# The first loads of a fused attention and gated-MLP kernel, moved from two issuing engines to one

## The chip, the cores and the metric

The kernel runs on one core of a Trainium2 chip. The metric is the device time of one execution in microseconds (us), the median over several executions. Beside it stands one execution recorded by the hardware profiler; all times inside the kernel come from that record and are counted from the start of its span.

The engines are named as in the profile: PE is TensorE (matmuls), PEld its weight loads, DVE is VectorE, ACT is ScalarE, POOL is GpSimd and SP is SyncE, which computes nothing here and issues DMAs. An entry such as SPq or ACTq is the issue of a DMA by that engine; L540 is line 540 of the kernel.

## What is computed

One sequence x of 2048 rows and 512 columns (bfloat16) is normalised row by row. A local attention (32 heads of 16 columns, 8 positions back at a stride of 2) and a gated MLP with spatial mixing both work on the normalised rows, and x is added to their sum. Cut to what matters here:

```
xn = layernorm(x)
q, k, v = xn @ wqkv                     # 512 x 1536; v is the last third
o = softmax(q . k over 8 dilated positions) applied to v
A = o @ wo
z = gelu(xn @ w_in)                     # 512 x 1792
g = w_sp @ layernorm(z[:, 896:]) + b_sp # mixing over the 2048 rows
B = (z[:, :896] * g) @ w_out
result = x + A + B
```

## The kernel before

The rows are cut into 16 blocks of 128 (block b is rows 128b to 128b + 127). The work goes in stages that overlap: the head, in which the blocks are loaded, normalised and transposed and the first products V and z2 are made; Q, K, the attention's logits and its softmax; z1; the mixing matrix (L982, the longest part); the output product (L1038 and L1047).

Each piece of work is a task with its engine, what it reads and writes, an estimated duration and a priority. A planner (`Plan.schedule`, L123) plays the tasks through and so fixes each engine's order; `Plan.emit` (L270) then writes the instructions with the semaphore waits that the reads and writes ask for. A DMA task has the engine that issues it as its engine. For some DMAs the planner doesn't work out when they land but is told it by a table of due times in nanoseconds, `land`, at L1094. The lists at L1078 to L1088 force an order by hand on top of that: the whole order of TensorE's tasks in the head, from the warm-up matmuls to the first chunk of Q and K, is one such list, and so is VectorE's.

What the head does, in order:

- TensorE runs warm-up matmuls on a constant (L582, `warm0` to `warm6`, six with 512 columns and then one with 128), which need no load.
- Block 0 of x (L563), block 1 and the next ones (`ld_x`, L536), and the weights of V in two halves (`ld_wv`, L540, 256 of the 512 input rows each) are loaded. Behind them come the two halves of the z2 part of w_in (L546 and L552, called w_in2 here), then block 4.
- For blocks 0 to 2, TensorE transposes the raw block with matmuls against an identity (`pe_tr`, L601, tasks `xTx0a` to `xTx2`); ScalarE copies the result from PSUM to SBUF (L628 for the first two quarters of block 0, L632 for the rest); TensorE multiplies it with V's weights (L704, tasks `V0_0`, `V0_0b` and so on: the first two with the first half of the weights, `V0_1` with the second). The eighth warm-up matmul, `warm7`, stands between block 0's transposes and `V0_0`. ScalarE scales V by the row's reciprocal deviation (L712); what the mean adds is corrected later.
- Meanwhile VectorE makes the statistics of each block (L621, L623, L636), GpSimd the reciprocal deviation (L638), and VectorE the normalised block (L650). Block 0's is transposed by TensorE (`xTr0`, also L601), that of every other block by a DMA transpose that SyncE issues (L644, `xTd1` on).
- TensorE then multiplies the normalised blocks with the second half of w_in (L836, `z2_0_0` on): the first half of block 0's columns needs the first half of w_in2, the second half of the columns the second, and block 1's needs `xTd1`.

Before the change, ScalarE issues block 0 and then block 1, and its next task is a four-element activation (L586), ahead of which it loads its function table. SyncE issues V's weights (both halves), blocks 2 and 3, w_in2's two halves, block 4, and later the DMA transposes. Each of the two engines issues its DMAs one after the other on a queue of its own (q10 for ScalarE, q1 for SyncE in the profile).

Of the kernel before, what the change touches and what calls it, by code (L numbers as in the profile page):

```python
# [346 lines left out]
def build_kernel(nc, A_x, A_wqkv, A_wo, B_x, B_w_in, B_w_sp, B_b_sp, B_w_out, out, report=False, emit=True):  # L347
# [14 lines left out]
    x2 = A_x[0]  # L362
# [48 lines left out]
    with ExitStack() as es:  # L411
# [5 lines left out]
        def A(name, n, o2_=0):  # L417
            return ar[:, off[name] + o2_: off[name] + o2_ + n]

        def AC(o_, dims):  # L420
            return bass.AP(tensor=ar, offset=o_, ap=[[AR, 128]] + [list(d) for d in dims])
# [91 lines left out]
        def dma(eng, fn, nbytes, chan, reads=(), writes=(), name="", xbar=False, prio=0.0, after=()):  # L513
            return T(eng, fn, reads=reads, writes=writes, name=name, prio=prio, after=after,
                     dma=dict(chan=chan, nbytes=nbytes, xbar=xbar, iss=(1270.0 if nbytes < 400000 else 2200.0) if xbar else None))
# [18 lines left out]
        def ld_x(b, eng="sp"):  # L534
            sl = b
            return dma(eng, lambda e: e.dma_start(A("xin", 512, 512 * sl), x2[128 * b:128 * b + 128, :]), 128 * 512 * 2,  # L536
                ("xin", sl), writes=[("xin", sl)], name="ldx%d" % b)

        def ld_wv(hf):
            dma("sp", lambda e: e.dma_start(AC(off["wv"] + 1024 * hf, [[512, 2], [1, 512]]),  # L540
                                            A_wqkv[256 * hf:256 * hf + 256, 1024:1536].rearrange("(c p) n -> p c n",
                                                                                               p=128)),
                256 * 512 * 2, ("wv", hf), writes=[("wv", hf)], name="ldwv%d" % hf)
# [13 lines left out]
        def ld_wqk(which, eng):  # L557
# [2 lines left out]
                A_wqkv[:, 512 * which: 512 * which + 512].rearrange("(c p) n -> p c n", p=128)),  # L560
                512 * 512 * 2, ("wqk", which), writes=[("wqk", which)], name="ld%s" % ("qk"[which]))

        dma("act", lambda e: e.dma_start(A("xin", 512), x2[0:128, :]), 128 * 512 * 2, ("xin", 0),  # L563
            writes=[("xin0", 0), ("xin0", 1)], name="ldx0")
        ld_x(1, "act")
        ld_wv(0)
        ld_wv(1)
        ld_x(2, "sp")
        ld_x(3, "sp")
# [508 lines left out]
        for names in (["warm%d" % wi for wi in range(NWARM)] +  # L1078
# [10 lines left out]
            for n0, n1 in zip(names, names[1:]):  # L1089
                if byname[n0] not in byname[n1].deps:  # L1090
                    byname[n1].odeps.add(byname[n0])

        plan.schedule(tol=4.0, dma_bw=285.0, dma_lat=1600.0, overlap=60.0,
                      land=dict(ldx0=3600.0, ldwv0=4120.0, ldx1=4550.0, ldwv1=5230.0, ldx2=5600.0, ldwin2a=7650.0, ldx3=6050.0,  # L1094
                                ldwin2b=8950.0, csa=75800.0, csb=78400.0, csc=83400.0, csr=86500.0, ldx4=9100.0, ldx5=18150.0, ldq=16300.0, xTd3=12130.0, ldk=17800.0, ldx6=18500.0, ldx7=18900.0, xTd4=13900.0, xTd1=9600.0, xTd2=10850.0, ldwin1=21500.0))
        if report:
            print("arena", AR, "fp", FR)
# [17 lines left out]
def bass_parallel_sum__sliding_local_dilated__mixer_gmlp__prompt_kernel(  # L1115
    nc, A_x, A_wqkv, A_wo, B_x, B_w_in, B_w_sp, B_b_sp, B_w_out, out
):
    build_kernel(nc, A_x, A_wqkv, A_wo, B_x, B_w_in, B_w_sp, B_b_sp, B_w_out, out)
# [28 lines left out]
```

## Time and profile before

| | |
|---|---|
| median of 3 runs | 236.16 us (235.97 to 236.21) |
| the profiled execution's own time | 236.12 us |
| its span | 234.9 us |
| TensorE busy | 98% of the span |
| VectorE busy | 88% |
| ScalarE busy | 41% |
| moved by SyncE's queue (q1) | 41.94 MB |
| moved by ScalarE's queue (q10) | 0.30 MB |

The profiled execution's time is longer than the span by what lies before the first and behind the last instruction that the span holds. Busy time counts an instruction from its start to its end, and since matmuls are pipelined, a busy TensorE can still run below its best rate. The chain of waits follows the last instruction back to whatever released it, step by step. Of a DMA the profile shows the instruction that issues it, on the issuing engine, and the time from there until it has landed.

### The profile page before, as it was taken

To read this page: it belongs to the slowest core of one execution; us is meant where nothing else is said; L and a number is where in the kernel's file an instruction comes from. 1 tells how busy PE (TensorE), PEld (TensorE's weight loads), DVE (VectorE), ACT (ScalarE), POOL (GpSimd) and SP (SyncE) were. 2 spreads that over 40 slices of the span, in tenths; PEclk is the share of its full clock that TensorE was granted. 3 is DMA by queue.
4 is the path that set the end of the run, shared out by engine and by line. 5 is a ranking of instruction groups with operands and counts; after the bars stand their busy time and mean duration, and the time that the engine had idled before them with its cause. 6 is when DMAs were issued, how large, how long until landed. Compare 5 with 4: busy or idle time off the path is not lost.

```text
span 234.9 us, 2982 instructions
## 1 busy us (share of the span) xinstructions
PE 230.9 (98%) x1107; PEld 109.0 (46%) x1127; DVE 207.2 (88%) x271; ACT 96.0 (41%) x144; POOL 29.3 (12%) x58
## 2 busy tenths in 40 slices
PE   8999999999999999999999999999999999999996
PEld 3545455544444444444444444444444444444443
DVE  4706899999999999999999999998899998999723
ACT  3798878888986589510020532011111111000000
POOL 2305640404261202000000000000000000000000
DMA  6769934999811275345299999999969959945442
GB/s 205 219 197 372 175 68 99 217 190 226 230 47 47 67 238 170 63 123 147 74 358 219 282 208 260 190 230 274 300 187 273 305 138 307 290 116 156 112 137 68
DMA packets 83991, 44.55 MB, mean 190 GB/s; under 512 B 56180, under 2 KB 83204, under 8 KB 83976
## 3 DMA queue, kind: packets, MB, share of 16 engines
q1 hardware_dynamic: 82744, 41.94, 70.6%
q0 software_dynamic: 800, 2.11, 2.9%
q10 hardware_dynamic: 432, 0.30, 0.4%
q8 instruction: 9, 0.15, 0.3%
q14 instruction: 6, 0.05, 0.1%
HBM read 26.62 MB, written 4.22 MB: 131 GB/s over the span
## 4 chain that ended last, share of the span: by engine, by line
PE 98%; issue 1%; DVE 0%; DVEq 0%
PE ps L982 41%; PE ps L728 12%; PE ps L836 10%; PE ps L882 10%; PE ps L1047 10%; PE ps L704 6%; PE ps L1038 6%; PE ps L582 1%; PE ps L772 1%; PE ps L601 1%; DVE arena L1053 0%; PE ps L783 0%; DVEq L325 0%
## 5 line engine op out<-in xcount | busy, mean ns | idle before, releaser
L982 PE MATMUL ps<-arena 128*128 128x512 bf16 x439 | 96.6, 379 | 0.5
L982 PEld LDWEIGHTS ps<-arena 128*128 128x128 bf16 x448 | 43.7, 98 | 53.1 <-issue 0.4
L990 ACT ACTIVATE arena<-ps 128x1024 bf16<-128x1024 f32 (+1 forms) x16 | 14.7, 917 | 76.9 <-PE ps L982 70.5
L749 DVE TENSOR_TENSOR arena<-arena 128x4096 bf16<-128x4096 bf16 x16 | 36.5, 2285 | 0.0
L1010 DVE TENSOR_TENSOR arena<-arena 128x4096 bf16<-128x4096 bf16 x16 | 36.5, 2286 | 0.0
L1013 DVE TENSOR_TENSOR arena<-arena 128x2048 bf16<-128x2048 bf16 (+1 forms) x32 | 30.1, 953 | 0.2
L728 PE MATMUL ps<-arena 128*128 128x512 bf16 x124 | 28.2, 379 | 0.3 <-issue 0.2
L754 DVE TENSOR_TENSOR arena<-arena 128x4096 bf16<-128x4096 bf16 x12 | 27.5, 2290 | 0.1
L1047 PE MATMUL ps<-arena 128*128 128x512 bf16 (+2 forms) x116 | 26.5, 366 | 0.1
L836 PE MATMUL ps<-arena 128*128 128x448 bf16 x128 | 25.5, 352 | 0.0
L882 PE MATMUL ps<-arena 128*128 128x512 bf16 x110 | 24.4, 379 | 0.1
L728 PEld LDWEIGHTS ps<-arena 128*128 128x128 bf16 x128 | 14.4, 113 | 13.3 <-ACT arena L718 0.4
L737 ACT ACTIVATE arena<-ps 128x1024 bf16<-128x1024 f32 x16 | 16.2, 1021 | 6.9 <-PE ps L728 6.8
L1053 DVE TENSOR_TENSOR arena<-ps,arena 128x512 bf16<-128x512 f32 (+2 forms) x17 | 11.2, 659 | 8.6 <-PE ps L1047 8.5
L836 PEld LDWEIGHTS ps<-arena 128*128 128x128 bf16 x128 | 12.5, 98 | 12.1
L1047 PEld LDWEIGHTS ps<-arena 128*128 128x128 bf16 x119 | 11.4, 98 | 12.8
L882 PEld LDWEIGHTS ps<-arena 128*128 128x128 bf16 x112 | 11.0, 98 | 13.2
L1038 PE MATMUL ps<-arena 128*128 128x512 bf16 (+2 forms) x68 | 16.6, 366 | 0.1
L704 PE MATMUL ps<-arena 128*128 128x512 bf16 x62 | 16.2, 391 | 0.1
L844 ACT ACTIVATE arena<-ps 128x896 bf16<-128x896 f32 x16 | 14.6, 913 | 3.4 <-PE ps L836 3.3
L621 DVE BATCH_NORM_STATS2 fpool<-arena 128x6 f32<-128x512 bf16 x16 | 10.7, 685 | 5.8 <-DMA arena<-in_A_x_dram 5.8
L888 ACT ACTIVATE arena<-ps 128x1024 bf16<-128x1024 f32 (+1 forms) x16 | 14.0, 919 | 4.4 <-PE ps L882 4.3
(65 smaller groups left out, 168.5 us busy)
## 6 DMA issues: line engine op xcount, KB each, us to landing
arena<-vscr SPq DMA_DIRECT2D x16, 1024.0 KB, 6.2
arena<-in_A_x_dram SPq DMA_DIRECT2D x30, 128.0 KB, 3.9
vscr<-arena POOLq DMA_DIRECT2D x16, 128.0 KB, 4.0
out_dram<-arena SPq DMA_DIRECT2D x15, 128.0 KB, 2.0
arena<-in_A_wqkv_dram SPq DMA_DIRECT2D x2, 512.0 KB, 4.5
arena<-in_B_w_in_dram SPq DMA_DIRECT2D x2, 448.0 KB, 5.1
arena<-in_B_w_in_dram SPq DMA_DIRECT2D x1, 896.0 KB, 8.3
arena<-in_B_w_out_dram SPq DMA_DIRECT2D x1, 896.0 KB, 5.6
```

Of the source, the lines that this page charges most:

```text
L704: last = t.matmul(P(bk, 512), A("xcT", 128, 512 * b + 128 * dc) if b < NRAW else xTv(b, dc), A("wv", 512, 512 * dc), start=(dc == 0), stop ...
L728: last = t.matmul(P(bk, 512, 512 * which), AC(off["wqk"] + 2048 * which + 512 * dc + c, [[4, 128]]), AC(off["xnT"] + dc * S + 512 * j, [[1 ...
L737: T("act", lambda a: a.activation(AC(qo, [[ko - qo, 2], [1, 512]]), P(bk, 1024).rearrange("p (t n) -> p t n", t=2), ACTF.Copy, scale=0.5), ...
L749: T("dve", (lambda pbv, qb, kb: lambda v: v.tensor_tensor(pbv, qb, kb, ALU.mult))(pbv, qb, kb), reads=rd, writes=[("pb", s_)], est=c_tt(40 ...
L754: T("dve", (lambda av, bv: lambda v: v.tensor_tensor(av, av, bv, ALU.add))(av, bv), reads=[("pb", 1)], writes=[("pb", acc)], est=c_tt(4096 ...
L836: last = t.matmul(P(bk, 448, 512 * hf), xTv(b, dc), AC(off["w_in2"] + 896 * dc + 448 * hf, [[1, 448]]), start=(dc == 0), stop=(dc == 3))
L882: last = t.matmul(P(bk, 512, 512 * i), AC(off["w_in1"] + 896 * dc + 128 * fc, [[1, 128]]), AC(off["xnT"] + dc * S + 512 * j, [[1, 512]]), ...
L982: last = t.matmul(P(bk, 512, 512 * i), AC(off["z2"] + FH * sh + 128 * fc, [[1, 128]]), AC(off["wT%d" % r_] + sh * 512, [[1, 512]]), start= ...
L1010: T("dve", lambda v: v.tensor_tensor(tv, tv, av, ALU.mult), reads=[("attn", b)], writes=[("Vs", sv)], est=c_tt(4096), name="pv%d" % b, pri ...
L1013: T("dve", (lambda n: lambda v: v.tensor_tensor(A("Vs", n, 4096 * sv), A("Vs", n, 4096 * sv), A("Vs", n, 4096 * sv + n), ALU.add))(n), wri ...
L1038: last = t.matmul(P(bk, cn), AC(off["OT"] + 512 * tb + 128 * cc, [[1, 128]]), AC(off["wo"] + 512 * cc + c0, [[1, cn]]), start=(cc == 0), s ...
L1047: last = t.matmul(P(bk, cn), AC(off["z1T"] + fc * S + 128 * tb, [[1, 128]]), AC(off["w_out"] + 512 * fc + c0, [[1, cn]]), start=False, sto ...
```

## The change

Block 0 and block 1 are issued by SyncE instead of ScalarE, and the order on SyncE is now block 0, V's weights first half, block 1, V's weights second half, and behind these, as before, blocks 2 and 3, w_in2's halves and block 4. ScalarE issues no load in the head. In the planner's table the due time of block 0 goes from 3600 to 3400; the others stay.

```diff
-        dma("act", lambda e: e.dma_start(A("xin", 512), x2[0:128, :]), 128 * 512 * 2, ("xin", 0),
+        dma("sp", lambda e: e.dma_start(A("xin", 512), x2[0:128, :]), 128 * 512 * 2, ("xin", 0),
             writes=[("xin0", 0), ("xin0", 1)], name="ldx0")
-        ld_x(1, "act")
         ld_wv(0)
+        ld_x(1, "sp")
         ld_wv(1)
         ld_x(2, "sp")
         ld_x(3, "sp")
...
-                      land=dict(ldx0=3600.0, ldwv0=4120.0, ldx1=4550.0, ldwv1=5230.0, ldx2=5600.0, ...
+                      land=dict(ldx0=3400.0, ldwv0=4120.0, ldx1=4550.0, ldwv1=5230.0, ldx2=5600.0, ...
```

More of the change, by code (lines that the diff above doesn't have):

```diff
@@ L1093, in build_kernel @@
         plan.schedule(tol=4.0, dma_bw=285.0, dma_lat=1600.0, overlap=60.0,
-                      land=dict(ldx0=3600.0, ldwv0=4120.0, ldx1=4550.0, ldwv1=5230.0, ldx2=5600.0, ldwin2a=7650.0, ldx3=6050.0,
+                      land=dict(ldx0=3400.0, ldwv0=4120.0, ldx1=4550.0, ldwv1=5230.0, ldx2=5600.0, ldwin2a=7650.0, ldx3=6050.0,
                                 ldwin2b=8950.0, csa=75800.0, csb=78400.0, csc=83400.0, csr=86500.0, ldx4=9100.0, ldx5=18150.0, ldq=16300.0, xTd3=12130.0, ldk=17800.0, ldx6=18500.0, ldx7=18900.0, xTd4=13900.0, xTd1=9600.0, xTd2=10850.0, ldwin1=21500.0))
```

## The prediction, made before the changed kernel was run

> **What bounds the kernel now.** I read the profile's head and its chain first, then TensorE's own timeline over the first 10 us, then the loads.
>
> ```profile
> span 234.9 us, 2982 instructions
> PE 230.9 (98%) x1107; PEld 109.0 (46%) x1127; DVE 207.2 (88%) x271; ACT 96.0 (41%) x144; POOL 29.3 (12%) x58
> PE 98%; issue 1%; DVE 0%; DVEq 0%
> ```
>
> TensorE is 98% of the chain that ended last. So nearly every wait that matters has to be a hole in TensorE's stream, and a load counts only if TensorE reaches its data before the data is there. The change touches loads that are all landed by 9.1 us, so I look for holes there. The next rows are from the timeline (start, length, instructions):
>
> ```profile
> 0.84 2.82 PE L582 MATMUL ps<-const-bfloat16-1.0 128*128 128x512 bf16 x7 [0.84 <-PEq L1132]
> 2.92 0.74 PE L582 MATMUL ps<-const-bfloat16-1.0 128*128 128x512 bf16 x2
> 3.54 0.69 DVE L621 BATCH_NORM_STATS2 fpool<-arena 128x6 f32<-128x512 bf16 x1 [2.35 <-DMA arena<-in_A_x_dram]
> 3.65 0.26 PE L601 MATMUL ps<-arena 128*128 128x128 bf16 x1
> 3.95 0.28 ACT L628 ACTIVATE arena<-ps 128x128 bf16<-128x128 f32 x1 [0.71 <-PE ps L601]
> 4.03 0.31 PE L582 MATMUL ps<-const-bfloat16-1.0 128*128 128x128 bf16 x1
> 4.34 0.21 PEld L704 LDWEIGHTS ps<-arena 128*128 128x128 bf16 x2 [0.27 <-issue]
> 4.37 0.58 PE L704 MATMUL ps<-arena 128*128 128x512 bf16 x1
> 5.18 0.63 PE L601 MATMUL ps<-arena 128*128 128x128 bf16 x4
> 5.61 0.85 PE L704 MATMUL ps<-arena 128*128 128x512 bf16 x2
> 6.03 0.42 PE L704 MATMUL ps<-arena 128*128 128x512 bf16 x1
> 6.29 0.39 PE L601 MATMUL ps<-arena 128*128 128x128 bf16 x4
> 6.51 1.03 PE L704 MATMUL ps<-arena 128*128 128x512 bf16 x4
> 8.46 4.70 PE L836 MATMUL ps<-arena 128*128 128x448 bf16 x24
> ```
>
> Matmul lengths overlap (they hold a pipeline tail), so I go by starts. Four things are seen. First, early 512-column matmuls are 0.43 us apart (5.61 to 6.03) and 128-column ones 0.11 (4 in 5.18 to 5.61); the matmul that starts at 6.03 is followed after 0.26 us, and the group from 8.46 needs 4.70/24 = 0.20 for 448 columns. So the rate doubles inside the matmul from 6.03: with 0.43 us for a slow and 0.22 for a fast one, 0.08 us of its 0.26 were slow, which puts the **rate step** at about 6.11. Second, the last warm-up matmul (128 columns, it starts at 2.92 + 0.43 = 3.35) gives the array free at 3.46; the first transpose of x block 0 starts at 3.65. These 0.19 us are a wait for block 0, which VectorE's statistics show as well (released by the DMA at 3.54). Third, a second hole lies between the last warm-up (4.03 + 0.11 = 4.14) and V's first matmul at 4.37: that one is the transpose's copy by ScalarE (3.95 to 4.23). Fourth, from 4.37 on TensorE runs through.
>
> Now the loads, first their issues (timeline), then issue to landing (DMA view, in windows holding one or two issues):
>
> ```profile
> 0.80 0.43 ACTq L563 DMA_DIRECT2D arena<-in_A_x_dram  x1
> 0.80 0.97 SPq L540 DMA_DIRECT2D arena<-in_A_wqkv_dram  x2
> 1.25 0.46 ACTq L536 DMA_DIRECT2D arena<-in_A_x_dram  x1
> 1.82 0.93 SPq L536 DMA_DIRECT2D arena<-in_A_x_dram  x2
> 2.79 0.43 SPq L546 DMA_DIRECT2D arena<-in_B_w_in_dram  x1
> 3.27 0.51 SPq L552 DMA_DIRECT2D arena<-in_B_w_in_dram  x1
> 3.82 0.51 SPq L536 DMA_DIRECT2D arena<-in_A_x_dram  x1
> ```
>
> ```profile
> arena<-in_A_wqkv_dram SPq DMA_DIRECT2D x1, 256.0 KB, 3.2
> arena<-in_A_x_dram ACTq DMA_DIRECT2D x1, 128.0 KB, 2.7
> arena<-in_A_wqkv_dram SPq DMA_DIRECT2D x1, 256.0 KB, 4.0
> arena<-in_A_x_dram ACTq DMA_DIRECT2D x1, 128.0 KB, 3.1
> arena<-in_B_w_in_dram SPq DMA_DIRECT2D x1, 448.0 KB, 5.5
> arena<-in_A_x_dram SPq DMA_DIRECT2D x1, 128.0 KB, 5.3
> arena<-arena SPq DMA_TRANSPOSE x1, 2.7
> ```
>
> Adding issue and landing time: block 0 lands at 3.5, V's first half at 4.0, block 1 at 1.25 + 3.1 = 4.35, the second half at 1.3 + 4.0 = 5.3, the second half of w_in2 at 3.27 + 5.5 = 8.8, block 4 at 3.82 + 5.3 = 9.1. They already land in the order of the change, though issued by two engines.
>
> **The change part by part.** (a) ScalarE loses two issues (0.43 and 0.46 us). Behind them stands only its table load and a four-element activation; its first copy waits for TensorE until 3.95. Worth nothing.
>
> (b) SyncE gains two issues. Its seven issues are (3.82 - 0.80)/6 = 0.50 apart, so block 0 goes at 0.80, V's first half at 1.30 (0.50 later than now), block 1 at 1.81 (0.56 later), the second half at 2.31, and all behind it about 1.0 later, up to block 4 at 4.82. Whether a later issue is a later landing depends on whether the DMA engines are the limit. The windows view (length, busy times, clock, DMA share, GB/s):
>
> ```profile
> 1.80:2.50 0.70, 0.70 (x4) 0.15 (x1) 0.00 (x0) 0.70 (x1) 0.00 (x0) 1.00 0.72 221
> 2.50:3.50 1.00, 1.00 (x4) 0.29 (x2) 0.00 (x0) 0.73 (x2) 0.00 (x0) 1.00 0.91 304
> 3.50:4.50 1.00, 0.97 (x8) 0.61 (x7) 0.89 (x3) 0.55 (x3) 0.00 (x0) 1.00 0.99 342
> 4.50:5.60 1.10, 1.10 (x6) 0.62 (x6) 1.03 (x5) 0.17 (x1) 0.57 (x1) 1.00 0.91 286
> 5.60:9.70 4.10, 4.10 (x27) 2.21 (x26) 3.30 (x12) 3.15 (x8) 1.76 (x3) 1.00 0.88 282
> ```
>
> From 2.5 on they are 88 to 99% busy: the bytes set the landings, not the issues. I assume the same stream of bytes in the new order. Running sums are 155 kB by 2.5, 459 by 3.5, 801 by 4.5, 1116 by 5.6. Block 0 (131 kB) has passed at 1.80 + 131/221 = 2.39, V's first half (393) at 3.28, block 1 (524) at 3.69, the second half (786) at 4.46. Today the second half lands 5.3 - 4.46 = 0.84 behind its bytes and block 1 4.35 - 3.69 = 0.66. With 0.75: **block 0 at 3.1 to 3.2, first half 4.0 to 4.1, block 1 4.4 to 4.5, second half 5.2 to 5.3**. Only block 0 moves: today its bytes share the engines with V's first half.
>
> [...]
>
> (c) TensorE. With block 0 there before 3.4, the first transpose follows the warm-ups at 3.46 instead of 3.65: 0.19 earlier. Right behind another matmul it takes 0.31 (like the one at 4.03), not 0.26, so it ends at 3.77 instead of 3.91. The gain left is 0.14: copy 3.81 to 4.09, V's first matmul at 4.23, if the first half has landed by about 4.15. Ends: 0.19 if the tail doesn't lengthen; 0 if the half lands at 4.3; and 4.5 (1.30 + 3.2, the later issue carried through) starts V at 4.6, 0.2 later than now. I take 0.14, the stream's value.
>
> (d) The rate step. Work moved forward by 0.14 in the slow part saves only half, if the step stays at 6.11: the second-half matmul that is 0.08 in at 6.11 today would be 0.22 in; its remaining half takes 0.10 and the next group starts at 6.22 instead of 6.29. **Gain 0.07 us.** If the step moved with the work it would be 0.14.
>
> (e) The next needs, 0.14 or 0.07 earlier than now:
>
> ```profile
> 5.50 0.25 PEld L704 LDWEIGHTS ps<-arena 128*128 128x128 bf16 x2
> 9.03 0.10 PEld L836 LDWEIGHTS ps<-arena 128*128 128x128 bf16 x1
> 9.79 0.10 PEld L836 LDWEIGHTS ps<-arena 128*128 128x128 bf16 x1
> 6.91 1.29 SPq L644 DMA_TRANSPOSE arena<-arena  x1
> ```
>
> V's second half is needed at 5.36 and lands at 5.2 to 5.3; the second half of w_in2 at 8.96 and lands at 8.8; the first transposed block (issued 6.91, 2.7 to landing, 9.6 to 9.65) at 9.72. All hold, the first and last by under 0.15. The order behind is unchanged: TensorE's list is written by hand up to Q's and K's first chunk, and the one due time that moves (block 0) is caught up by the unmoved 5230 of V's second half.
>
> The sum: 236.12 (profiled, span 234.9 and 1.2 around it) - 0.07 = 236.05. The median of the runs, 236.16, is 0.04 higher, so I forecast **236.09**. A measurement can tell about 0.2%, 0.47 us: my forecast is no measurable change.
>
> **The rivals.**
> 1. *The gain is eaten at V's weights.* If the halves land as late as their issues move (4.5 and, worse than the stream's, 5.5 or more), V starts 0.2 late in the slow part: 236.16 + 0.1 = 236.25. If block 0 isn't held by sharing, nothing moves: 236.16. For it: margins of 0.1. Against: 91 to 99% busy DMA engines. Either way within 0.47.
> 2. *The later issues reach w_in2 and the transposed blocks.* Carried through in full, the w_in2 half lands at 9.8 for a need at 8.96, and the transposed block at 10.65 for 9.72: 0.93 - 0.07 = 0.86 slower, 237.0. If a third carries, 0.25: 236.4. For it: the engines are only 88% busy behind 5.6. Against: block 4 waits 5.3 us after its issue while block 0 needs 2.7.
> 3. *The rate step comes later* (the other side). If what brings the step is an unbroken stretch of matmuls, and V's second half is late so that TensorE stands from about 5.4, the slow part could begin anew: it now lasts 0.84 to 6.11 = 5.27, so the step would be at 10.7, 4.6 us more at half rate, 2.3 slower: 238.4. It decides once the wait at 5.4 exceeds what is tolerated today, the holes of 0.19 and 0.23. Against: the step came in spite of both.
> 4. *The step comes earlier* because the hole at 3.46 closes. With all behind 3.46 at full rate, V's second half (5.3) holds TensorE to 5.4, so xT of block 2 starts at 5.83, 0.46 earlier; but w_in2 (8.8 against 8.57) and the transposed block (9.65 against 9.33) take back 0.32: 236.0. Over 0.47 only if the loads come earlier too: 235.6.
>
> [...]
>
> **How the numbers follow.** Forecast 0.47; rival 1 0.19; rival 2 0.17, nearly half of it beyond 0.47; rival 3 0.10; rival 4 0.07, of which 0.05 beyond. Within 0.2%: 0.47 + 0.19 + 0.09 + 0.02 = 0.77; slower 0.08 + 0.10 = 0.18; faster 0.05. The range 235.8 to 236.7 leaves out rival 3, the top of rival 2 (0.04) and rival 4's far end (0.05).
>
> **What would show it.** Right: the first transpose at 3.46 and the statistics before 3.3; V's first matmul near 4.23; the rate step still near 6.11; the group of 24 at 8.39; then every start 0.07 earlier to the end. Wrong: V's weight load behind 4.34 (rival 1), a hole before 9.0 or 9.8 (rival 2), matmuls 0.43 apart behind 6.2 (rival 3), or 0.22 apart before 6.0 (rival 4).

## The result, and the profile after

The changed kernel is slower: **237.61 us** median of 7 runs (236.66 to 239.09) against 236.21 of 7 runs of the kernel before on the same chip (235.97 to 236.42). The ratio of the means is **1.0064, 95% interval 1.0038 to 1.0091**. The spread matters as well: 2.4 us from the lowest to the highest run, where the kernel before has 0.45. The profiled execution took 237.97 us.

The head of the page and the chain of the changed kernel:

```profile
span 236.7 us, 2982 instructions
PE 231.3 (98%) x1107; PEld 108.8 (46%) x1127; DVE 207.6 (88%) x271; ACT 96.0 (41%) x144; POOL 29.3 (12%) x58
PE 94%; DMA 3%; SPq 1%; issue 1%; DVE 0%; DVEq 0%
```

The busy times hardly say anything. The chain does: before it was 98% TensorE, and now 3% are DMA and 1% SyncE's issuing. So TensorE waited for loads, and the timeline (start, length, instructions; the wait ahead of a row in brackets) shows where:

```profile
0.80 0.39 SPq L563 DMA_DIRECT2D arena<-in_A_x_dram  x1
1.25 0.41 SPq L540 DMA_DIRECT2D arena<-in_A_wqkv_dram  x1
1.71 0.46 SPq L536 DMA_DIRECT2D arena<-in_A_x_dram  x1
2.21 0.43 SPq L540 DMA_DIRECT2D arena<-in_A_wqkv_dram  x1
2.69 0.95 SPq L536 DMA_DIRECT2D arena<-in_A_x_dram  x2
2.97 0.69 DVE L621 BATCH_NORM_STATS2 fpool<-arena 128x6 f32<-128x512 bf16 x1 [1.77 <-DMA arena<-in_A_x_dram]
3.46 0.63 PE L601 MATMUL ps<-arena 128*128 128x128 bf16 x4
3.68 0.43 SPq L546 DMA_DIRECT2D arena<-in_B_w_in_dram  x1
4.16 0.51 SPq L552 DMA_DIRECT2D arena<-in_B_w_in_dram  x1
4.22 1.01 PE L704 MATMUL ps<-arena 128*128 128x512 bf16 x2
5.03 0.63 PE L601 MATMUL ps<-arena 128*128 128x128 bf16 x4
6.78 0.60 PE L704 MATMUL ps<-arena 128*128 128x512 bf16 x2 [1.12 <-DMA arena<-in_A_wqkv_dram]
7.22 0.39 PE L601 MATMUL ps<-arena 128*128 128x128 bf16 x4
9.60 0.93 PE L836 MATMUL ps<-arena 128*128 128x448 bf16 x4
10.86 1.86 PE L836 MATMUL ps<-arena 128*128 128x448 bf16 x8 [0.33 <-DMA arena<-in_B_w_in_dram]
```

Up to 5.4 all goes as predicted: statistics at 2.97, first transpose at 3.46, V's first matmul at 4.22. Then TensorE has nothing from 5.03 + 4 x 0.107 = 5.46 to 6.78: V's second half isn't there. The first matmul behind it that can be compared is block 2's transpose, 7.22 against 6.29: 0.93 late. w_in2's matmuls begin at 9.60 instead of 8.46 (1.14 late). The second half of their columns begins at 10.86; before, they began 4 x 0.19 behind 8.46, at 9.22 (1.64 late). The group of 24 is torn in pieces. The list of waits in the first 13 us names the loads (us in total, times, longest):

```profile
PEld ps L704 <- DMA arena<-in_A_wqkv_dram: 1.7, 2, 1.4
PEld ps L836 <- DMA arena<-in_B_w_in_dram: 1.3, 2, 0.8
PE ps L704 <- DMA arena<-in_A_wqkv_dram: 1.1, 1, 1.1
PEld ps L836 <- DMA arena<-arena: 0.4, 1, 0.4
```

Three holes: V's second half, w_in2 (twice), the transposed block 1. From 11.8 on every matmul starts 1.82 later than before, up to the last at 234.57 against 232.75. That is the whole difference of the two profiled executions (237.97 - 236.12 = 1.85); the medians differ by 1.40.

From issue to landing (DMA view; KB, us):

```profile
arena<-in_A_x_dram SPq DMA_DIRECT2D x1, 128.0 KB, 2.1
arena<-in_A_wqkv_dram SPq DMA_DIRECT2D x1, 256.0 KB, 2.7
arena<-in_A_x_dram SPq DMA_DIRECT2D x1, 128.0 KB, 2.5
arena<-in_A_wqkv_dram SPq DMA_DIRECT2D x1, 256.0 KB, 4.5
arena<-in_B_w_in_dram SPq DMA_DIRECT2D x1, 448.0 KB, 5.9
```

Block 0 lands at 0.80 + 2.1 = 2.9, V's first half at 3.95, block 1 at 4.2, all early enough. The second half needs 4.5 us from 2.21, so 6.7; it was forecast for 5.2 to 5.3. The windows show where the time goes (length, busy times, clock, DMA share, GB/s; a packet counts where it starts, so a share can pass 1):

```profile
1.80:2.50 0.70, 0.70 (x4) 0.15 (x2) 0.00 (x0) 0.48 (x2) 0.00 (x0) 1.00 0.65 214
2.50:3.50 1.00, 1.00 (x5) 0.44 (x4) 0.53 (x1) 0.00 (x0) 0.00 (x0) 1.00 0.96 281
3.50:4.50 1.00, 0.97 (x8) 0.63 (x6) 0.71 (x4) 0.70 (x3) 0.35 (x1) 1.00 0.73 158
4.50:5.60 1.10, 1.10 (x6) 0.52 (x4) 1.03 (x4) 0.03 (x1) 0.36 (x2) 1.00 0.59 170
5.60:9.70 4.10, 2.94 (x20) 1.44 (x20) 2.57 (x9) 2.22 (x6) 1.07 (x2) 1.00 1.01 316
```

Between 3.5 and 5.6, where the stream ran at 342 and 286 GB/s before, it runs at 158 and 170. By 5.6 the changed kernel has moved 150 + 281 + 158 + 187 = 776 kB, the kernel before 1116. The missing 340 kB are one us of stream. All nine loads have been issued by 5.22, V's second half by 2.64, and still packets of 1024 bytes that take 46 ns in the stream take up to 0.82 us at 3.9. I call this **running dry**: the stream thins where V's second half follows on block 1. That it thins because the work reaches the DMA engines late is an inference, which the experiments test.

### The profile page after: what moved, and what is told of

It is laid out like the page before. It is cut to its first block, busy times and chain, and to the rows that moved or that the text cites. A ratio compares the mean times of both kernels' runs of the same rounds, so it can differ in the third digit from the quotient of the medians.

```text
span 236.7 us, 2982 instructions
## 1 busy us (share of the span) xinstructions
PE 231.3 (98%) x1107; PEld 108.8 (46%) x1127; DVE 207.6 (88%) x271; ACT 96.0 (41%) x144; POOL 29.3 (12%) x58
## 3 DMA queue, kind: packets, MB, share of 16 engines
HBM read 26.62 MB, written 4.22 MB: 130 GB/s over the span
## 4 chain that ended last, share of the span: by engine, by line
PE 94%; DMA 3%; SPq 1%; issue 1%; DVE 0%; DVEq 0%
PE ps L982 41%; PE ps L728 12%; PE ps L882 10%; PE ps L836 10%; PE ps L1047 10%; PE ps L1038 6%; PE ps L704 5%; DMA arena<-in_B_w_in_dram 3%; PE ps L772 1%; SPq L536 1%; DVE arena L1053 0%; SPq L540 0%; SPq L546 0%; SPq L563 0%; PE ps L783 0%
```

## The experiments

All medians and their ranges, with the ratio of the means to the kernel before on the same chip (its medians there: 236.04, 236.02, 236.03 and 235.94, for each four of these rows in turn):

| run | median us (range, runs) | ratio, 95% interval |
|---|---|---|
| e1_wv1_act | 237.45 (237.21 to 237.69, 4) | 1.0056, 1.0039 to 1.0072 |
| e2_wv1_act_late | 237.34 (236.52 to 238.23, 10) | 1.0051, 1.0033 to 1.0070 |
| e3_x1_act | 237.14 (236.46 to 238.56, 8) | 1.0052, 1.0031 to 1.0072 |
| e4_x0_act | 237.11 (236.16 to 237.87, 10) | 1.0037, 1.0021 to 1.0053 |
| e5_merged | 237.06 (236.48 to 238.47, 10) | 1.0051, 1.0030 to 1.0071 |
| e6_before_tiny_sp | 237.86 (236.67 to 239.89, 10) | 1.0075, 1.0048 to 1.0102 |
| e7_hold | 238.18 (one run) | |
| e8_after_tiny_act | 237.80 (237.56 to 238.75, 4) | 1.0081, 1.0052 to 1.0110 |
| e9_before_one_tiny | 237.00 (236.12 to 238.44, 12) | 1.0048, 1.0028 to 1.0069 |
| e10_before_x23 | 236.43 (235.91 to 237.14, 12) | 1.0020, 1.0008 to 1.0031 |
| e11_x0_act_wv | 237.00 (236.72 to 238.07, 7) | 1.0051, 1.0032 to 1.0069 |
| e12_wv_merged | 238.14 (237.04 to 239.24, 6) | 1.0087, 1.0062 to 1.0112 |
| e13_fill_after | 237.16 (236.97 to 238.09, 6) | 1.0058, 1.0042 to 1.0075 |
| e14_fill_e12 | 237.23 (236.98 to 237.37, 5) | 1.0052, 1.0040 to 1.0064 |
| e15_tiny_before_win2 | 236.17 (235.71 to 236.31, 11) | 1.0002, 0.9993 to 1.0011 |
| e16_tiny_act | 236.77 (236.35 to 238.43, 11) | 1.0053, 1.0032 to 1.0074 |

The theory at the start: one engine that issues everything supplies too slowly, by its queue or by its issue time. The second form became the **lead theory**: a load needs some 2 us from its issue until the DMA engines can work at it, and one issued too short before they come to it leaves them dry. The 2 us are the author's estimate; in the traces the first packet of w_in2, known by its 896 bytes, starts 2.1 us behind its issue in the kernel before (4.86 for 2.79) and 2.3 in the changed one (5.99 for 3.68), and the very first packet of all 1.0 us behind its issue (1.81 for 0.80, the changed kernel). Its lead is the time from its issue to the moment at which they have worked through all that stands in front of it. The rivals were the single queue as such, ScalarE's table load (it now runs at 0.80 instead of 1.74, beside the first loads), and crowding by the loads issued behind.

**One load back to ScalarE at a time.** Each of four runs moves one load of the changed kernel.

```diff
-        ld_wv(1)                 # e1, e2 (e2: behind the activation)
+        ld_wv(1, "act")
...
-        ld_x(1, "sp")            # e3
+        ld_x(1, "act")
...
-        dma("sp", ... ("xin", 0) # e4
+        dma("act", ... ("xin", 0)
```

> Only the second half of V's weights goes back to ScalarE, issued at 0.80; SyncE keeps block 0, first half, block 1 and the rest. Supply theory (one issuing engine can't hand out packets fast enough in the first 6 us, whatever the order): SyncE's queue has 512 KB less ahead of w_in2 in two steps, the second half lands by 5.3, no hole ahead of V0_1, 236.0 to 236.4. Lateness theory (the second half lands late only because it is issued at 2.21 instead of 1.31): it lands by 4.5, 236.0 to 236.3. Table theory (ScalarE's table load, at 0.80 instead of 1.74, disturbs the loads): the load now begins at 1.25, so about half of the loss stays, 236.9.

> As the one before, but ScalarE issues the second half behind its table load, at about 2.2, the same time as in the changed kernel. Supply theory: it lands by 5.4 all the same, 236.0 to 236.4. Lateness theory: a DMA issued at 2.2 lands at 6.5 to 6.8 on this queue too, V0_1 waits as in the changed kernel, 237.3 or more. Table theory: the table load is at 0.80 as in the changed kernel, 237.3 or more.

> Only block 1 goes back to ScalarE (issued at 0.80); SyncE has block 0, first half, second half at 1.71, then the rest 0.5 earlier than in the changed kernel. Supply theory: 128 KB less through SyncE ahead of the second half, which lands at 5.0 to 5.6, 236.1 to 236.6. Lateness theory: issue half a step earlier, landing about 6.0, 236.8 to 237.1. Table theory: 236.9.

> Only block 0 goes back to ScalarE; SyncE has first half, block 1, second half at 1.75, then the rest. Supply theory: 384 KB through SyncE up to block 1, so the second half is the first that can come late, 5.2 to 5.8, 236.2 to 236.8; block 0 shares the engines again and lands at 3.4 to 3.5. Lateness theory: second half about 6.0, 236.8 to 237.1. Table theory: 236.9.

Measured: 237.1 to 237.5 all four, so none brings the time back. The supply theory's numbers are missed in all four, e1 misses every theory's, and the lateness theory comes near in e3 and e4 (236.8 to 237.1, the half at about 6.0). In e1 V's second half is there at 3.91, and the loss only moves: TensorE stands 0.71 ahead of V's first half and 1.16 ahead of w_in2. In e2 ScalarE's queue didn't wait for the table load, so its issue came at 1.08, not late, and the run doesn't test a late issue; V's first matmul then waited until 5.10. In e3 and e4 the second half, issued at 1.71 and 1.81, still lands at 6.40 and 6.14. Two queues are not enough, then: the loss doesn't need a single queue.

The windows of e4 show a late landing with little of a dry stream ahead of it:

```profile
3.50:4.50 1.00, 0.97 (x8) 0.63 (x7) 0.93 (x4) 0.69 (x3) 0.00 (x0) 1.00 0.99 328
4.50:5.60 1.10, 0.69 (x6) 0.31 (x4) 1.03 (x4) 0.40 (x3) 0.65 (x2) 1.00 0.76 229
```

Up to 4.5 it is nearly as full as before (342), and by 5.6 1048 kB have moved (before 1116, in the changed kernel 776). Packets of w_in2 (896 bytes each in the trace) start at 5.07, while V's second half lands only at 6.14. So a part of the half lags by a us behind packets of a later load. Why is not shown.

**Fewer issues (e5).** Blocks 0 and 1 in one load, blocks 2 and 3 in one, all on SyncE:

```diff
-        dma("sp", ... x2[0:128, :]) ... name="ldx0")
+        dma("sp", ... x2[0:256, :].rearrange("(c p) n -> p c n", p=128)) ... name="ldx0")
         ld_wv(0)
-        ld_x(1, "sp")
         ld_wv(1)
-        ld_x(2, "sp")
-        ld_x(3, "sp")
+        dma("sp", ... x2[256:512, :].rearrange("(c p) n -> p c n", p=128)) ... name="ldx2")
```

> All on SyncE, but blocks 0 and 1 are one DMA and blocks 2 and 3 another: first x pair, V's halves, second x pair, w_in2's halves, block 4. Seven issues as in the kernel before, where the changed one has nine; the bytes and their order are nearly those of the change. Lead theory (an issue has to be given at least 2.1 us before the DMA engines get to it, and every 128 KB issue costs SyncE 0.48 us while its bytes take 0.36, so nine issues use up the lead): the second half is issued at 1.7 and needed by the engines at 3.5, V_1's wait shrinks from 1.1 to under 0.4, 235.9 to 236.6. Queue theory (one queue alone supplies too slowly, however it is cut): 237.2 or more. Table theory (table load at 0.80): 237.2 or more.

Measured 237.06: the lead theory's number is missed (235.9 to 236.6), and its rivals' (237.2 or more) by little. V's second half is still issued at 1.81, half a us later than before, and lands at 6.32. And its profile, of the slowest of the ten runs (238.47), shows something new:

```profile
6.46 1.01 PE L704 MATMUL ps<-arena 128*128 128x512 bf16 x2 [0.63 <-DMA arena<-in_A_wqkv_dram]
7.26 0.63 PE L601 MATMUL ps<-arena 128*128 128x128 bf16 x4
7.69 1.91 PE L704 MATMUL ps<-arena 128*128 128x512 bf16 x4
9.39 0.63 PE L601 MATMUL ps<-arena 128*128 128x128 bf16 x4
9.82 1.15 PE L704 MATMUL ps<-arena 128*128 128x512 bf16 x4
```

Groups of four 128-column matmuls take 0.63 at half rate and 0.39 at full rate; here they still take 0.63 at 9.39, and four 512-column ones 1.91 instead of 1.03. The rate step comes at about 10.1 (the last group is 0.12 longer than the 1.03 of full rate, so 0.24 of it ran at half), not 6.1: **rival 3 of the prediction, seen once**.

**Issue time alone (e6).** The kernel before, two engines issuing, with two loads of 512 bytes, which nothing reads, ahead of SyncE's list:

```diff
+        dma("sp", lambda e: e.dma_start(ar[0:16, off["tg"]:off["tg"] + 16], x2[0:16, 0:16]), 512, ...)
+        dma("sp", ...)                                   # the second
         dma("act", ... ("xin", 0)
```

> The kernel before with two loads of 512 bytes (into space that w_in's z1 part overwrites later) ahead of SyncE's others: only the time of two issues is added, 0.9 us, the bytes stay, two engines still issue, and the table load stays at 1.74. Lead theory: V's halves are issued at 1.7 and 2.2, the first lands 4.6 to 5.0, the second 5.8 or later, 236.8 to 238. Queue theory: only the shift of the first half counts, 236.2 to 236.5. Table theory: 236.0 to 236.5.

Measured 237.86, as slow as the change. Its windows and two rows of its timeline:

```profile
2.50:3.50 1.00, 1.00 (x5) 0.45 (x4) 0.63 (x1) 0.71 (x2) 0.00 (x0) 1.00 0.67 178
5.60:6.50 0.90, 0.34 (x2) 0.00 (x0) 0.00 (x0) 0.56 (x2) 0.11 (x1) 1.00 0.77 119
```

```profile
4.65 0.59 PE L704 MATMUL ps<-arena 128*128 128x512 bf16 x2 [0.68 <-DMA arena<-in_A_wqkv_dram]
7.35 0.40 PE L601 MATMUL ps<-arena 128*128 128x128 bf16 x4 [1.41 <-DMA arena<-in_A_x_dram]
```

The two loads are 1 KB, where the kernel before moves 1116 kB by 5.6; what they add is 0.9 us of issue time ahead of V's weights (issued from 1.71 instead of 0.80). The dry stretches are now 178 GB/s at 2.5 to 3.5 and 119 at 5.6 to 6.5, and TensorE waits behind each. SyncE's issue time alone reproduces the loss, with two issuing engines and, but for 1 KB, the same bytes. But the lead theory has only the time right. It forecast V's halves at 4.6 to 5.0 and at 5.8 or later; they landed at 4.51 and 5.29, the second as early as before although it was issued at 2.17. What came late was block 2 (7.31, before 5.64).

**Crowding and the table load (e7, e8).** e7 holds block 2 until block 1 has landed, and a list of orders keeps the loads behind it; e8 is the changed kernel with two 512-byte loads on ScalarE, so that its table load is at 1.71, nearly as before (1.74).

```diff
-                ("xin", sl), writes=[("xin", sl)], name="ldx%d" % b)      # e7
+                ("xin", sl), reads=[("xin", 1)] if b == 2 else [], writes=[("xin", sl)], name="ldx%d" % b)
...
+        dma("act", ... 512, ("tiny", 0), ...); dma("act", ... 512, ("tiny", 1), ...)   # e8
```

> The changed kernel with block 2 and all behind it on SyncE held back until block 1 has landed (about 4.25). The kernel gets slower, 238.5 to 240, as blocks 2 and 3 and w_in2 come 1.5 us later; what it tells is when V's second half lands with nothing issued behind it. Lead and queue theory: still 6.0 or later. Crowding theory (the issues behind it slow its supply): by 5.3.

> The changed kernel with two loads of 512 bytes issued by ScalarE ahead of its table load, which so starts at 1.74 as in the kernel before. Lead, queue and crowding theory: as the changed kernel, 237.2 to 238. Table theory: 236.0 to 236.4.

In e7 (238.18, a little under the 238.5 expected) nothing stands behind V's second half until 4.77, and it still lands at 5.88, with the engines 46 to 80% busy from 4.0 to 4.8: 0.9 earlier than in the changed kernel, but 0.6 later than before, and between the two theories' numbers. So crowding has a part at most, by one run. e8: 237.80, the half at 6.41. The table load falls.

**How much, and where (e9 to e12).** e9 is e6 with one small load. e10 is the kernel before with blocks 2 and 3 in one load (the second edit of e5). e11 is the changed kernel with block 0 on ScalarE and block 1 behind both halves. e12 is the changed kernel with V's weights in one load of 512 KB and blocks 2 and 3 in one.

```diff
-        ld_x(1, "sp")            # e11
-        ld_wv(1)
+        ld_wv(1)
+        ld_x(1, "sp")
...
-        ld_wv(0)                 # e12
-        ld_x(1, "sp")
-        ld_wv(1)
+        dma("sp", ... A_wqkv[0:512, 1024:1536].rearrange("(c p) n -> p c n", p=128)), 512 * 512 * 2, ...)
+        ld_x(1, "sp")
```

> The kernel before, with one load of 512 bytes (into memory that nothing reads) ahead of SyncE's first; ScalarE still issues blocks 0 and 1. Every SyncE issue moves back by about 0.46, half of what the run with two did. Lead theory (an issue needs some 2.0 to 2.1 us before the DMA engines come to it): the second half of V's weights, issued at 1.77 behind blocks 0 and 1, is reached at 3.4 to 3.7, a lead of 1.6 to 1.9, so the engines run dry by 0.2 to 0.5 there and once more at w_in2: 236.4 to 237.2, between the kernel before and the run with two. A fixed price for any change of SyncE's list: as with two, 237.8. A price by the number of engines that issue: two issue here, 236.0 to 236.3.

> The kernel before, with blocks 2 and 3 in one load of 256 KB: SyncE issues six loads for seven, w_in2 and block 4 go 0.5 us earlier. Lead theory: w_in2's lead grows from 3.1 to 3.6 us, no engine runs dry behind V's weights, its halves land at 7.1 to 7.5 and 8.4 to 8.7; TensorE had no hole of its own there before, so no gain that can be measured, 235.9 to 236.2; block 2 now lands with block 3, at 6.1 to 6.3, and TensorE wants it at 6.29, so up to 0.2 of loss if it lands late. A theory by which bigger loads are slower in themselves: 236.5 or more.

> The changed kernel with block 0 on ScalarE at 0.80 and both halves of V's weights at 0.80 and 1.31 on SyncE, as before; block 1 behind them at 1.8, then blocks 2 and 3, w_in2 and block 4, each 0.5 later than before. Lead theory: the second half is back at its old issue time and is reached at 2.9 to 3.2 with 131 KB less in front of it, which is a lead of 1.6 to 1.9 too: the engines may run dry for 0.2 to 0.4, but that lands it at 4.9 to 5.3, ahead of its need at 5.4; block 1 then lands at 5.3 to 5.8 for a need at about 5.2; w_in2, issued at 3.3, is reached at about 6.0, lead 2.6: no dry spell. 236.2 to 236.7. If the loss hangs on SyncE's issuing one load more, whatever the order: 237.1, as with block 0 alone moved to ScalarE in the changed order.

> All loads on SyncE, V's weights in one load of 512 KB behind block 0, then block 1, blocks 2 and 3 in one, w_in2's halves, block 4: seven issues at 0.8, 1.3, 1.8, 2.3, 2.8, 3.3, 3.8. As many issues as in the run with blocks 0 and 1 merged (237.06), but 512 KB stand in line by 1.3 and not 1.8, and the issues behind them have 1.5 us of bytes in front. Lead theory: no dry spell behind 2.5; V's weights land whole at 4.8 to 5.1, TensorE waits there for some 0.6 in the slow part (worth 0.3) and no more; block 1 at 5.1 to 5.4, w_in2 at 7.3 to 7.7: 236.2 to 236.6. A price by the number of SyncE's issues: 237.0 again.

e9 gives 237.00, between none and two, as the lead theory has it. Against its detail, the dry spell lies ahead of V's first half (5.04 instead of 4.00), not the second (5.78). e11 misses the theory's number: the second half is back at 4.75, but w_in2 lands at 9.67. My reckoning of when the engines come to it (6.0) was wrong; with 131 + 524 + 393 kB in front at 340 GB/s (342 from 3.5 to 4.5 in the kernel before) from 1.9 on it is 5.0, a lead of 1.7. e10 goes against the theory: it gives w_in2 more lead, and gets 236.43, slower than before (1.0008 at least) and near the 236.5 of a rival by which bigger loads are slower in themselves, which no run tests further. Its windows:

```profile
4.50:5.60 1.10, 1.10 (x8) 0.48 (x6) 1.03 (x5) 0.23 (x2) 0.57 (x1) 1.00 1.23 295
5.60:6.50 0.90, 0.90 (x9) 0.44 (x8) 0.90 (x4) 0.77 (x3) 0.66 (x1) 1.00 0.78 233
```

The kernel before, in the second of them:

```profile
5.60:6.50 0.90, 0.90 (x8) 0.50 (x7) 0.90 (x4) 0.65 (x2) 0.66 (x1) 1.00 1.05 363
```

363 GB/s flowed from 5.6 to 6.5 before, 233 here, although w_in2 was issued at 2.32, some 2.6 us ahead of its turn. From 4.5 to 5.6 the DMA share is 1.23 for 295 GB/s, where the kernel before has 0.91 for 286: packets took longer there, which counts as busy. Lead is not all of it.

e12 misses by more, 238.14, and not by w_in2, which is there at 7.94 and 9.11; V's weights land at 5.37, behind the 4.8 to 5.1 expected. Timeline:

```profile
5.51 1.01 PE L704 MATMUL ps<-arena 128*128 128x512 bf16 x2 [1.31 <-DMA arena<-in_A_wqkv_dram]
7.59 0.63 PE L601 MATMUL ps<-arena 128*128 128x128 bf16 x4
8.02 1.73 PE L704 MATMUL ps<-arena 128*128 128x512 bf16 x4
9.59 0.39 PE L601 MATMUL ps<-arena 128*128 128x128 bf16 x4
```

TensorE waits from 4.0 to 5.5 for V's weights, and then runs at half rate until about 9.45 (of the 1.57 from 8.02 to 9.59, three matmuls take 0.43 each and the fourth 0.29). Again the late step.

**Is the late step made by the hole (e13, e14)?** Three 512-column matmuls on constants fill it, with every load left where it is. In e13 they stand ahead of block 1's transposes in the changed kernel, in e14 behind the last warm-up in e12's order.

```diff
                 last = None                                              # e13
+                last = [t.matmul(P(bk, 512), ones[:, 0:128], ones[:, 0:512], start=True, stop=True)
+                        for i in range(3 * (name == "xTx1"))]
                 for dc in dcs:
...
-            T("pe", (lambda bw, n_: lambda t: t.matmul(P(bw, n_), ones[:, 0:128], ones[:, 0:n_], ...   # e14
+            T("pe", (lambda bw, n_, wi: lambda t: [t.matmul(P(bw, m_), ones[:, 0:128], ones[:, 0:m_], ...)
+                     for m_ in [n_] + [512] * 3 * (wi == NWARM)][-1])(bw, n_, wi),
```

> The changed kernel with three 512-column matmuls on constants (their result is overwritten, and read by nothing) ahead of block 1's transposes: TensorE is busy from 5.03 to about 6.3 where it stood from 5.41 to 6.78; all loads and the lists of the other engines are as in the changed kernel. [...] If the loss is the late loads alone: the same median as the changed kernel, 237.4 to 237.8, and executions up to 239 as before.

> The kernel with V's weights in one load (238.14, V's first matmul at 5.51 behind a hole of 1.5 us, clock step at about 9.4) with three 512-column matmuls on constants behind the last warm-up, inside that hole; nothing else differs. If the hole puts the clock step off: the step is back at about 6.1, which is 3.3 us less at half rate, 1.65 less, 236.4 to 236.8. If the step has another cause: 238.1 again, with matmuls 0.43 apart until 9.3.

e14: 237.23 (236.98 to 237.37) against 238.14 (237.04 to 239.24). Timeline:

```profile
3.83 0.88 PE L582 MATMUL ps<-const-bfloat16-1.0 128*128 128x128 bf16 x4
5.68 0.59 PE L704 MATMUL ps<-arena 128*128 128x512 bf16 x2 [0.97 <-DMA arena<-in_A_wqkv_dram]
6.11 0.39 PE L601 MATMUL ps<-arena 128*128 128x128 bf16 x4
```

The last warm-up and the three fillers, from 3.83, are through within 0.88, so they already ran at full rate, and so does all behind 5.68: V's weights come even later than in e12, and the time is 0.9 better. 236.4 to 236.8 was expected, so the size was missed, but a price of the loads alone would have left 238.1. In this profile full rate came before the fillers began, so it doesn't show that they brought it; that the late executions are gone rests on the runs alone, five up to 237.37 against six up to 239.24. e13: 237.16, highest 238.09, where 237.4 to 237.8 and up to 239 were expected of the late loads alone, against 237.61 and 239.09 in the changed kernel. The intervals overlap; in the changed kernel the late step is likely and not shown.

The step also moves without a long hole ahead of it. Up to 3.46 TensorE does the same in all these kernels, and the starts of its matmuls put full rate at 3.6 in e6, 3.8 in e14, 4.3 in e3, 5.1 in e10, 6.0 in e11, 6.1 in the kernel before and 6.7 in e13 and e15. Two rows that hold the step, of e6 and of e15 (0.63 would be all half rate, 0.39 all full rate):

```profile
3.46 0.45 PE L601 MATMUL ps<-arena 128*128 128x128 bf16 x4
```

```profile
6.33 0.54 PE L601 MATMUL ps<-arena 128*128 128x128 bf16 x4
```

So 6.11 was one execution's value and no property of the kernel, and two profiled executions can differ by the step alone. Only e5 and e12 lie beyond this range. And a hole doesn't always put the step off: in the changed kernel and in e8 TensorE stands from 5.46 to 6.78 and to 6.45, and runs at full rate right behind.

**Where a late issue costs nothing (e15, e16).** One 512-byte load in the kernel before, ahead of w_in2 on SyncE (e15) or ahead of block 0 on ScalarE (e16).

```diff
         ld_x(3, "sp")
+        dma("sp", ... 512, ("tiny", 0), ...)      # e15
         ld_win2a()
...
+        dma("act", ... 512, ("tiny", 0), ...)     # e16
         dma("act", ... ("xin", 0)
```

> The kernel before with one load of 512 bytes between block 3 and w_in2 on SyncE: w_in2's halves and block 4 are issued 0.46 later (3.25, 3.73, 4.28), all before them as before. The DMA engines come to w_in2 at about 5.1, so its lead falls from 2.3 to 1.85 us. Lead theory: the engines run dry there by 0.3 to 1.5, w_in2 lands at 7.8 to 9.2 for a need at 8.46, its second half and the first transposed block are late by 0.2 to 1.3 behind it: 236.2 to 237.2. If a lead of 1.85 is enough: 236.0.

> The kernel before with one load of 512 bytes ahead of ScalarE's block 0: blocks 0 and 1 are issued 0.46 later (1.25, 1.71), SyncE's list as before. Lead theory: SyncE's loads keep the DMA engines supplied (V's first half is reached at 1.9, its second half at about 2.7 with no block in front, lead 1.4: a short dry spell of up to 0.3), and blocks 0 and 1 land at 3.6 to 4.1 and 4.5 to 5.0, so block 0 holds the first transpose by up to 0.45 in the slow part: 236.1 to 236.6. If every later issue had a price of its own, as on SyncE: 237.0.

e15 is as fast as before (1.0002, 0.9993 to 1.0011), and w_in2 lands at 7.59, earlier than the lead theory's 7.8 to 9.2, for a need at 8.46. So neither a late issue nor a small load has a price of its own here. But the same half at the same issue time (3.26 and 3.27) and behind the same bytes needs 4.3 us here and 6.4 in e11:

```profile
arena<-in_B_w_in_dram SPq DMA_DIRECT2D x1, 448.0 KB, 4.3
```

```profile
arena<-in_B_w_in_dram SPq DMA_DIRECT2D x1, 448.0 KB, 6.4
```

The first row is e15's, the second e11's, whose profiled execution was the slowest of its seven. So the dry spells differ in size, and from execution to execution at that: the changed kernel and e13 issue the same loads at the same times (within 0.01 us), and the same half lands at 9.55 in the one and at 8.33 in the other. e16 moves nothing on SyncE and loses 0.83, more than the lead theory had (236.1 to 236.6): blocks 0 and 1 land at 4.08 and 5.68, and TensorE waits for both. Its eleven runs fall in **two groups**, seven at 236.35 to 236.98 and four at 238.08 to 238.43. The middles (236.65 and 238.3) are 1.65 us apart, which is 3.3 us at half rate; the profiled execution, of the lower group, is at full rate by 4.2. The step of e5 (10.1) and e12 (9.45) comes 4.0 and 3.3 behind that of the kernel before (6.11), and 3.4 and 2.8 behind the latest of the others (6.7). What sets the time of the step is not shown.

## Why the prediction was wrong, point by point

- **Step (a), right.** ScalarE's lost issues gain nothing.
- **Step (c), right.** First transpose 3.46 (forecast 3.46), V's first matmul 4.22 (forecast 4.23).
- **Step (b), the failed step.** "The bytes set the landings, not the issues" was read from engines 88 to 99% busy. But that share belonged to the order in which two engines issue: with the same bytes in the new order, 340 kB fewer have moved by 5.6, and the second half lands at 6.74, not at 5.2 to 5.3. The prediction priced the later issues at nothing; in e6 0.9 us of issue time alone, ahead of SyncE's list, costs 1.8 us (237.86 against 236.02). The landings in all runs with the two halves apart:

| issue of V's second half | landed |
|---|---|
| 0.81, 1.08 (e1, e2, by ScalarE) | 3.91, 4.74 |
| 1.31 to 1.32 (before, e10, e11, e15, e16) | 4.75 to 5.30 |
| 1.71 to 1.81 (e3, e4, e5) | 6.14 to 6.40 |
| 2.21 to 2.22 (changed kernel, e8, e13) | 6.37 to 6.74 |
| 2.22, nothing issued behind it until 4.77 (e7) | 5.88 |
| 1.74, behind one small load (e9) | 5.78 |
| 2.17, behind two small loads (e6) | 5.29 |

From the second row to the third, half a us of issue costs 0.8 to 1.7 us of landing; but the last row was issued as late as in the changed kernel and landed as early as before, so the issue time doesn't set the landing alone. On SyncE the next issue follows 0.45 to 0.47 us behind a load of 0.5 KB and 0.46 to 0.52 behind one of 128 KB, which passes in 131/342 = 0.38, so each block put ahead on the same engine delays all that follows. The mistake was to carry a rate over from one order to another without asking whether each load is still issued early enough for it. For w_in2 no order by issue time shows (its first half, issued at 2.32, 2.79, 3.26, 3.27, 3.68, lands at 8.06, 7.51, 7.59, 9.67, 9.55): how a later issue thins the stream, and what else does, stays open.
- **Step (d), not tested.** In the changed kernel's profile the rate step falls into the hole (5.46 to 6.78); no 0.07 could be seen beside 1.4. It took 6.11 for a step that stays where it is; over the profiles it falls anywhere from 3.6 to 6.7, so no gain of this size can be worked out from one execution.
- **Step (e), wrong with (b).** All three margins called safe were broken: V's second half by 1.4, w_in2's halves and the transposed block behind it.
- **The rivals.** Rival 1 named the place, V's weights, and gave 0.1 for a half at 5.5; it came at 6.74. Rival 2 named the path; its full carry, 237.0, was the nearest to 237.61, but it took a late issue to carry through at most one to one. Rival 3 is real: seen in e5 and e12, and likely in e16's upper group, at 1.65 instead of the 2.3 reckoned, since the late step comes some 3.3 us later and not a whole new slow part of 4.6. It came with a late load for TensorE, so it was no rival beside the others but a second price of theirs, and the range left both out. Rival 4's early step is seen too (3.6 to 5.1 in e6, e14, e3 and e10), and brought no version under the kernel before.

No version beat the kernel before: e15 equals it, all others came out slower, e7 in its one run.

## What to carry to other kernels

A busy DMA share (0.88 to 0.99 from 2.5 on in the kernel before) showed here that the loads were issued early enough in that order, not that they would be in another (0.73 and 0.59 from 3.5 to 5.6 in the changed kernel): before a load moves to another engine's list, reckon for each load when the engines come to it and when it is issued, and keep the lead that it has today. That is a caution and no formula: the lead didn't foretell the landings here. At the start of this kernel two engines that issue side by side are worth some 0.46 us per load (the next issue on SyncE follows 0.45 to 0.52 behind), and small loads spend it (e6, e9, e16). A hole in TensorE's first microseconds went with two costs in e5 and e12, the waiting (0.63 and 1.31) and a later rate step (at 10.1 and 9.45), and with the waiting alone in the changed kernel's profile; where a load can be late there, filling the hole is worth a try (0.9 us from e12 to e14).

## What the runs showed of the hardware that was not expected

- From the first issue to the first packet pass 1.06 us in the kernel before (0.80 to 1.86) and 1.01 in the changed one (0.80 to 1.81). Packets of 1024 bytes that take 46 ns in the stream take up to 0.82 us where it runs dry (the changed kernel, at 3.9), and w_in2's of 896 bytes, 41 ns in the stream, up to 1.6 us (the changed kernel).
- Ahead of the rate step 512-column matmuls start 427 ns apart, behind it 216 (the kernel before, from 1.22 to 3.35 and from 6.51 to 7.38), while the granted clock in the windows is 1.00 in both parts (1.8 to 5.6 and 5.6 to 9.7).
- Full rate begins at 3.6 to 6.7 us in profiled executions whose TensorE work is the same up to 3.46, and at 9.45 and 10.1 in two.
- With losses at the start times scatter more: 2.4 us from lowest to highest for the changed kernel, 3.2 for e6, 0.45 to 1.2 for the kernel before in its five sets of runs, one execution of 237.74 aside.
